# The last head group's values in two long bursts, on one core

## The chip, the cores and the metric

The kernel runs on one core of one Trainium2 chip. The metric is the time of one execution on the device, in microseconds (us). Three runs of the kernel before took 708.56 to 709.26 us, median 708.99.

## The reference

A sequence of 2048 rows of 512 numbers goes through two branches, which a gate mixes:

```
qkv = (x @ wqkv), 32 heads of 16
scores = q @ k.T / 4, kept where 0 <= query - key < 256
a = (softmax(scores) @ v) @ wo
b = (sigmoid(x @ w_gate) * (x @ w_up)) @ w_down        # 1376 hidden columns
g = sigmoid((x * gate_w).sum(-1))
out = g * a + (1 - g) * b
```

## The kernel before

**First phase.** The heads are taken in 8 groups of 4. The loop over `u` goes through 128 blocks of 128 rows (16 per group) and some more. At each `u`, four times (`hh`, one per head), TensorE multiplies a score tile with queries down the partitions (`s_part`), which VectorE scans for its row maxima, and nine blocks later (`LAG`) one with keys down the partitions (`st_part`), whose maxima are already in the operands, and which ScalarE turns into probabilities (`exps`). GpSimd masks the edges (`mask_p`). From `u` = 128 on there are no more score tiles to scan. Between them `turns` puts pieces of the gate, up and tail projections (`gu`, `tp`), pairs of half-array multiplications; the list `sizes` says how many pairs go into each gap. Where they end, VectorE transposes a tail result (`tail_post`) and the queue stores it.

**Values.** Groups 0 to 6 multiply probabilities with values in bursts, at every eighth `u` from 17 on (`pv_wide`): two steps of 512 queries, keys in halves of 64 so that half blocks outside the window are left out, into four PSUM banks (tags `pv`, `st`, `st`, `s`). Each step's two banks are then added: ScalarE copies one, VectorE adds the other. The last group (`u` from 121) is done otherwise: at `u` = 125, 129, 133 and 137 a visit (`pv_part`) multiplies one step with all 128 keys at once into the one bank `pv`, and ScalarE copies it (`o_take`). Its probabilities stand in `pbuf` alone, so that `pwide`, a part of the tile `V`, is free for loads of the second phase.

**PSUM.** The eight banks are shared by tag: `s` 2, `st` 2, `misc` 3, `pv` 1. A tile with a tag takes the bank that has been free longest.

**Second phase.** 44 steps (4 chunks of 512 rows, 11 of hidden columns): sigmoid on ScalarE, product on VectorE, a split in a high and a low part on both, 12 multiplications on TensorE. Step `n` reads what `h_load(n)` has brought to one of eight places of `V`; `H_LOAD` says at which `u` steps 0 to 6 are loaded, later ones seven steps ahead. `o_load` and `o_scale` bring the heads' outputs with the reciprocals of their sums (`rec_scratch`).

**Order.** TensorE, ScalarE, VectorE and the queue of transfers (SP) work in the order in which the code is written; the queue waits at a transfer until what it needs is done.

Of the kernel before, what the change touches and what calls it, by code (L numbers as in the profile page):

```python
# [43 lines left out]
NWIDE = NG - 1  # L44
# [3 lines left out]
GAPS = [3] * 12 + [2] * 3  # L48
# [11 lines left out]
SUMS = {129: 0, 131: 1, 134: 2}  # L60
# [5 lines left out]
H_LOAD = {126: (0,), 130: (1, 2), 134: (3, 4), 137: (5, 6)}  # L66
# [3 lines left out]
def gated_mix_kernel(  # L70
# [77 lines left out]
    with ExitStack() as actx:  # L148
# [225 lines left out]
        def s_part(u, hh):  # L374
            g, i = divmod(u, NB)
            s = g * NC + i // 4
            if i % 4 == 0 and hh == 0:
                mxs[s] = spool.tile([P, HG, 4], F32, tag="mx", name=f"mx{s}")
            k0 = max(0, i - 2)
            tag = "st" if u < LAG and hh >= 2 else "s"  # L380
            if PVLAG < u <= NB * NWIDE + LAG and (u - LAG) % WIDE == 0 and hh == 1:
# [46 lines left out]
        homes = (((0, 1), (9, 1), (3, 2), (4, 2)), ((0, 1), (3, 1), (9, 2), (10, 2)))  # L428

        def p_home(u):  # L430
            if u // NB >= NWIDE:
                s0, step = homes[u // 4 % 2][u % 4]
                return pbuf, 2 * s0, 2 * step
            w = u % WIDE
            if w < 5:
                return pbuf, 6 * w, 2
            return pwide, 24 if w == 5 else 12 * (u // WIDE % 2) + 6 * (w - 6), 2

        def p_blk(u, hh, a, n):
            buf, s0, step = p_home(u)  # L440
            if step == 2:
                return buf[:, s0 + 2 * a:s0 + 2 * (a + n), hh]
            pairs = buf.rearrange("p (s c) h t -> p s c h t", c=2)
            a = s0 // 2 + a * (step // 2)
            return pairs[:, a:a + (n - 1) * (step // 2) + 1:step // 2, :, hh]

        def p_run(u, hh, half, k, e):
            buf, s0, _ = p_home(u)
            return buf[HB * half:HB * half + HB, s0 + k:s0 + e, hh]

        def st_part(u, hh):
            g, j = divmod(u, NB)
            tag = "s" if u + LAG >= NU and hh >= 2 else "st"
            k8 = u % WIDE * HG + (hh ^ 1)
            if 2 <= u < NB * NWIDE and k8 % 3 == 1 and 4 <= k8 < WIDE * HG - 2:
                tag = "pv"
            pt = ps.tile([P, 3 * P], F32, tag=tag, name=f"st{u}_{hh}", bufs=1 if tag == "pv" else 2)
            lhsT = blk(g, j, hh, 1)
            last = min(NB, j + 3)
            for q, e in pieces(g, j, last):  # L460
# [5 lines left out]
            out = p_blk(u, hh, 0, n)  # L466
            seen = "p (k t) -> p k t" if len(out.shape) == 3 else "p (b k t) -> p b k t"
            exps.append(nc.scalar.activation(  # L468
                out, pt[:, 0:n * P].rearrange(seen, t=HB, **({} if len(out.shape) == 3 else {"k": 2})),
                AF.Exp, scale=SCALE,  # L470
            ))

        def mask_p(u):
            buf, s0, step = p_home(u)
# [4 lines left out]
            if u % NB + 2 < NB:  # L479
                old = buf[:, s0 + 2 * step:s0 + 2 * step + 2]  # L480
# [8 lines left out]

        def pv_part(s, bank):  # L490
            g, c = divmod(s, NC)
            q0 = 4 * c
            j0 = max(0, q0 - 2)
            for j in range(j0, q0 + 4):
                q, e = max(j, q0), min(j + 3, q0 + 4)
                for hh in range(HG):
                    v = (j * HG + hh) * VW
                    w = min(32, NB * HG * VW - v)
                    mm(
                        bank[32 * hh:32 * hh + w, (q - q0) * P:(e - q0) * P],  # L500
                        vt[:, v:v + w],
                        p_blk(g * NB + j, hh, q - j, e - q),
                        start=j == j0, stop=j == q0 + 3, skip_group_check=True,
                        tile_position=(0, 32 * hh),
                    )
# [30 lines left out]
        def o_take(s, bank):  # L536
            g, c = divmod(s, NC)
            ob = cpool.tile([P, CH], F32, tag="sp", name=f"ob{s}", bufs=5)
            nc.scalar.copy(ob, bank)
            for hh in range(HG):  # L540
                h = g * HG + hh
                later.append((oT_d[h * DH:(h + 1) * DH, c * CH:(c + 1) * CH], ob[32 * hh:32 * hh + DH]))
            later.append((sum_d[c, g * HG:(g + 1) * HG], ob.rearrange("(h r) f -> r h f", r=32)[DH]))

        def o_home(s):
            old = 12 * ((s // 2 + 1) % 2)
            return pwide[:, old:old + 4].rearrange("p c h t -> p (c h t)")

        def o_sum(s, n, banks):
            home = o_home(s)[:, n * CH:(n + 1) * CH]  # L550
# [4 lines left out]
        def o_store(s):  # L555
            g, c = divmod(s, NC)
            both = o_home(s)
# [222 lines left out]
        def turns():  # L780
# [3 lines left out]
            sizes = GAPS2 + GAPS2 * (NB * NWIDE // WIDE - 1) + GAPS2[:5] + GAPS[5:] + GAPS[0:12]  # L784
            sizes += [6] * 14
            for size in sizes:
                for _ in range(size):
# [4 lines left out]
                    for half, v in enumerate((t, t - SHIFT)):  # L792
                        if 0 <= v < n_rest * k3:
# [3 lines left out]
                            if k == 0 and n in ended and (size > 5 or len(exps) < ended[n] + 3):  # L797
                                after(ins, exps[ended[n]])
# [29 lines left out]

        def h_load(n):
            c, f = steps[n]  # L830
            if f < NFM:
                nc.sync.dma_start(hv[:, n % 8], gu_d[:, f, :, c * CH:(c + 1) * CH].rearrange("w p t -> p w t"))
# [26 lines left out]
        def h_src(n, w):  # L859
            c, f = steps[n]  # L860
            return (hv[:, n % 8, w] if f < NFM else tail_home(c, f, w))[0:FCH[f]]
# [32 lines left out]
        def sums_load(c):  # L894
            sm[c] = cpool.tile([P, D], F32, tag="draw", name=f"sm{c}", bufs=2)[:, 0:P]
            nc.sync.dma_start(sm[c], flat(sum_d, c))

        def sums_invert(c):
            t = sm.pop(c)
            nc.vector.reciprocal(t, t)  # L900
            return flat(rec_d, c), t
# [17 lines left out]

        U_WIDE = NB * NWIDE + LAG  # L920
# [7 lines left out]
        for u in range(N):  # L928
# [18 lines left out]
            def transfers():  # L947
                if mark and visits.get(u) != 2:
# [35 lines left out]
            for hh in range(HG):  # L984
                wide = visits.get(u) == 2
                if hh == 0 and u in visits:
                    s2 = (u - PVLAG) // 4 - wide
                    pv = ps.tile([P, CH], F32, tag="pv", name=f"pv{s2}", bufs=1)
                    if wide:
                        banks = [[pv], []]  # L990
                        for n, tag in ((0, "st"), (1, "st"), (1, "s")):
                            banks[n].append(ps.tile([P, CH], F32, tag=tag, name=f"pv{s2}_{tag}{n}", bufs=2))
                        pv_wide(s2, banks)
                    else:
                        pv_part(s2, pv)
# [10 lines left out]
                if hh == 0 and wide:  # L1006
# [4 lines left out]
                    max_load((u - 5) // 4)  # L1011
# [11 lines left out]
                elif hh == 0 and u in visits:  # L1023
                    evac.append(lambda s2=s2, pv=pv: o_take(s2, pv))
                if hh == 2 and mark:
                    transfers()
                long = LAG <= u < U_WIDE
# [11 lines left out]
                if hh == 0 and wide:  # L1039
# [43 lines left out]
            if u - 2 in SUMS:  # L1083
                behind.append(lambda c=SUMS[u - 2]: later.append(sums_invert(c)))
# [66 lines left out]
        for n, (c, f) in enumerate(steps):  # L1151
# [19 lines left out]
            if n == 3:  # L1171
                run_dmas(later)
                sums_load(NC - 1)
            if n == 6:
                last_sums = sums_invert(NC - 1)
            if n == 7:
                nc.sync.dma_start(*last_sums)
# [91 lines left out]
```

## Time and profile before

| | |
|---|---|
| median of 3 runs | 708.99 us |
| the profiled execution | 708.45 us, of it 706.5 us span |
| TensorE, VectorE, ScalarE busy | 99%, 71%, 62% |
| the last group's visits begin at | 491.86, 506.11, 518.98, 533.01 us |
| first multiplication of the second phase | 540.74 us |

Times in the trace are counted from the start of the span. A busy TensorE also holds the filling and emptying of its pipeline, so small stops are read from the starts of its instructions.

### The profile page before, as it was taken

Reading aid. Unit: us, or ns where it says so; the run is one execution under the profiler, and the core shown is the slowest. Engines: PE = TensorE matmul, PEld = TensorE weight load, DVE = VectorE, ACT = ScalarE, POOL = GpSimd, SP = SyncE. Lnnn points to the kernel's source line nnn. Section 1 sums busy time; section 2 is a strip of 40 time slices with the busy share of each in tenths; the row PEclk is TensorE's granted clock in tenths of the full one; section 3 lists DMA queues with packets and bytes.
Section 4 is the critical chain, followed back from the end, with each engine's and each line's share of the span. In section 5 each row is a group of like instructions: output and inputs, shape, how many; then the busy total and the mean of one; then the engine's idle time right before and its main releaser. Section 6 shows DMA issues by size and latency. Waiting matters only on the chain.

```text
span 706.5 us, 20062 instructions
## 1 busy us (share of the span) xinstructions
PE 702.5 (99%) x7545; PEld 608.8 (86%) x7545; DVE 498.6 (71%) x1486; ACT 435.3 (62%) x889; POOL 171.7 (24%) x254
## 2 busy tenths in 40 slices
PE   9999999999999999999999999999999999999998
PEld 7888889998899988889888988988888888888886
DVE  5368877777777776777777777786747768567481
ACT  6423777677677677767767767765676645435241
POOL 6200333233233233323323323332341000000000
PEclk9999999999999999999999999999999999999999
DMA  8466635646445365462655626664569969678531
GB/s 307 118 196 196 218 127 181 204 145 208 159 166 184 135 207 180 159 231 80 216 174 180 214 85 216 210 206 122 174 198 261 273 169 233 181 185 244 146 67 60
DMA packets 102832, 127.38 MB, mean 180 GB/s; under 512 B 45750, under 2 KB 62390, under 8 KB 102736
## 3 DMA queue, kind: packets, MB, share of 16 engines
q1 hardware_dynamic: 102592, 125.98, 58.3%
q8 instruction: 59, 0.97, 0.6%
q14 instruction: 37, 0.30, 0.1%
q10 hardware_dynamic: 144, 0.13, 0.1%
HBM read 71.80 MB, written 51.13 MB: 174 GB/s over the span
## 4 chain that ended last, share of the span: by engine, by line
PE 99%; DVE 0%; issue 0%
PE gu L296 29%; PE pj L296 12%; PE st L461 6%; PE s L386 6%; PE tp L687 6%; PE pd L99 5%; PE pd L98 5%; PE pd L100 5%; PE pv_st L516 4%; PE vh L724 4%; PE pv_s L516 3%; PE pa L98 2%; PE pa L100 2%; PE pa L99 2%; PE pv L516 2%; PE vps L586 2%
## 5 line engine op out<-in xcount | busy, mean ns | idle before, releaser
L392 DVE CUSTOM_DVE_ANT_0 junk<-s,mask 128x384 f32<-128x384 f32 (+2 forms) x512 | 271.8, 531 | 103.9 <-PE st L461 38.1
L296 PE MATMUL gu<-xh,w 64*128 64x512 f32 x1152 | 270.3, 391 | 0.0
L468 ACT ACTIVATE pbuf<-st 128x384 f32<-128x384 f32 (+2 forms) x344 | 165.5, 490 | 61.6 <-PE st L461 30.5
L296 PE MATMUL gu<-xl,w 64*128 64x512 f32 x576 | 182.4, 389 | 0.0
L461 PE MATMUL st<-ring 64*128 64x384 f32 (+2 forms) x536 | 164.7, 324 | 0.0
L386 PE MATMUL s<-ring 64*128 64x384 f32 (+2 forms) x536 | 162.9, 322 | 0.0
L296 PEld LDWEIGHTS gu<-xh,w 64*128 64x128 f32 x1152 | 151.2, 184 | 10.1
L475 POOL TENSOR_SCALAR_AFFINE_SELECT pbuf<-pbuf 128x512 f32<-128x512 f32 x86 | 58.1, 676 | 274.4 <-ACT pbuf L468 260.1
L386 PEld LDWEIGHTS s<-ring 64*128 64x128 f32 x536 | 94.8, 184 | 14.0 <-DVE mx L392 2.7
L461 PEld LDWEIGHTS st<-ring 64*128 64x128 f32 x536 | 95.8, 184 | 7.9 <-issue 1.2
L296 PEld LDWEIGHTS gu<-xl,w 64*128 64x128 f32 x576 | 88.6, 184 | 3.0
L468 ACT ACTIVATE V<-st 128x384 f32<-128x384 f32 (+2 forms) x168 | 72.2, 439 | 29.3 <-PE s L386 16.4
L296 PE MATMUL pj<-xl,wqh 64*128 64x512 f32 (+1 forms) x228 | 79.2, 389 | 0.0
L296 PE MATMUL pj<-xh,wqh 64*128 64x512 f32 (+1 forms) x228 | 79.2, 389 | 0.0
L296 PE MATMUL pj<-xh,wql 64*128 64x512 f32 (+1 forms) x228 | 69.6, 388 | 0.0
L99 PE MATMUL pd<-ring,hb 128*128 128x512 f32 x160 | 62.3, 389 | 0.0
L100 PE MATMUL pd<-ring,hb 128*128 128x512 f32 x160 | 62.3, 389 | 0.0
L98 PE MATMUL pd<-ring,hb 128*128 128x512 f32 x160 | 62.3, 389 | 0.0
L94 ACT CAST hb<-V 128x512 fp32r<-128x512 f32 x40 | 24.9, 622 | 58.3 <-DVE V L887 45.2
L481 POOL TENSOR_SCALAR_AFFINE_SELECT pbuf<-pbuf 128x512 f32<-128x512 f32 x84 | 56.0, 666 | 0.0
L647 ACT COPY sp<-gu 128x512 f32<-128x512 f32 x72 | 42.2, 586 | 9.6 <-PE gu L296 6.7
L475 POOL TENSOR_SCALAR_AFFINE_SELECT V<-V 128x512 f32<-128x512 f32 x42 | 27.8, 661 | 70.0 <-ACT V L468 49.2
(154 smaller groups left out, 1374.5 us busy)
## 6 DMA issues: line engine op xcount, KB each, us to landing
gu_scratch<-sp SPq DMA_DIRECT2D x72, 256.0 KB
V<-gu_scratch SPq DMA_DIRECT2D x36, 512.0 KB
ring<-stack_scratch SPq DMA_DIRECT2D x56, 256.0 KB
stack_scratch<-sh SPq DMA_DIRECT2D x14, 512.0 KB
stack_scratch<-sl SPq DMA_DIRECT2D x14, 512.0 KB
ring<-stack_scratch SPq DMA_DIRECT2D x14, 512.0 KB
guraw<-in_wgu_dram SPq DMA_DIRECT2D x18, 256.0 KB
v_scratch<-V SPq DMA_DIRECT2D x4, 1088.0 KB
```

The costliest lines, as they stand in the source:

```text
L98: mm(ps, lh, rh, start=first, stop=False)
L99: mm(ps, lh, rl, start=False, stop=False)
L100: mm(ps, ll, rh, start=False, stop=last)
L296: return mm(pt, (wl if w == 2 else wh)[r, d], (xl if w == 1 else xh)[r, d, c * CH:(c + 1) * CH], start=k == 0 and not second, stop=k == 3 ...
L386: mm(pt[:, (k - k0) * P:(e - k0) * P], lhsT, blk(g, k, hh, 1, e - k), start=k == k0, stop=e == i + 1, skip_group_check=True,)
L392: nc.vector.tensor_tensor_reduce(junk[:, 0:n], pt[:, 0:n], mask[:, 3 * P - n:], scale=1.0, scalar=NEG, op0=ALU.add, op1=ALU.max, accum_out ...
L461: mm(pt[:, (q - j) * P:(e - j) * P], lhsT, blk(g, q, hh, 0, e - q), start=q == j, stop=e == last, skip_group_check=True,)
L468: exps.append(nc.scalar.activation(out, pt[:, 0:n * P].rearrange(seen, t=HB, **({} if len(out.shape) == 3 else {"k": 2})), AF.Exp, scale=S ...
L475: nc.gpsimd.affine_select(buf[:, s0:s0 + 2], buf[:, s0:s0 + 2], pattern=[[HB, 2], [0, HG], [1, HB]], compare_op=ALU.is_ge, fill=0.0, base= ...
L481: nc.gpsimd.affine_select(old, old, pattern=[[-HB, 2], [0, HG], [-1, HB]], compare_op=ALU.is_gt, fill=0.0, base=0, channel_multiplier=1,)
L516: mm(bank[32 * hh:32 * hh + w, o + k * HB:o + e * HB], vt[HB * half:HB * half + HB, v:v + w], p_run(g * NB + j, hh, half, k, e), start=fir ...
L687: return mm(tp[b][:, 0:TW], (xl if w == 1 else xh)[r, d, b * P:(b + 1) * P], tw[d][int(w == 2)][r, 0:TW], start=k == 0 and not second, sto ...
```

## The change

The last group is treated as the others: a burst at `u` = 129 and one at `u` = 137 instead of four visits, its probabilities in `pbuf` and `pwide` as runs. The scores' banks follow the rule of the other groups up to `u` = 127, and the list of gaps runs on in the pattern of the other groups, then 9 gaps of 6 pairs and 6 of 5. The four steps of the maxima at `u` = 125 are spread over the gaps before it. The last burst's sums go to two tiles of their own. Since `pwide` is in use until the end, step 0 is loaded at `u` = 131, steps 1 and 2 at 134 and 135 into corners of the x tiles, steps 3 to 6 at 137 behind the burst; sums of steps 2 and 3 are inverted together in the second phase.

```diff
-NWIDE = NG - 1
-GAPS = [3] * 12 + [2] * 3
-SUMS = {129: 0, 131: 1, 134: 2}
+SUMS = {131: 0, 133: 1}
-H_LOAD = {126: (0,), 130: (1, 2), 134: (3, 4), 137: (5, 6)}
+H_LOAD = {131: (0,), 134: (1,), 135: (2,), 137: (3, 4, 5, 6)}
...
         def p_home(u):
-            if u // NB >= NWIDE:
-                s0, step = homes[u // 4 % 2][u % 4]
-                return pbuf, 2 * s0, 2 * step
...
         def st_part(u, hh):
-            tag = "s" if u + LAG >= NU and hh >= 2 else "st"
+            tag = "s" if u + LAG >= NU and hh % 2 else "st"
-            if 2 <= u < NB * NWIDE and k8 % 3 == 1 and 4 <= k8 < WIDE * HG - 2:
+            if 2 <= u < NU - LAG and k8 % 3 == 1 and 4 <= k8 < WIDE * HG - 2:
                 tag = "pv"
...
-            sizes = GAPS2 + GAPS2 * (NB * NWIDE // WIDE - 1) + GAPS2[:5] + GAPS[5:] + GAPS[0:12]
-            sizes += [6] * 14
+            sizes = GAPS2 * (NU // WIDE - 2) + GAPS2[:4 * (WIDE - 1)] + [6] * 9 + [5] * 6
...
+        def h_home(n, w):
+            if 0 < n < 3:
+                return slot(n - 1, w, 1).bitcast(F32)
+            return hv[:, n % 8, w]
...
-        visits = {u: 2 for u in range(PVLAG + 4, U_WIDE + 1, WIDE)}
-        visits.update({u: 1 for u in range(U_WIDE + 4, N, 4)})
+        visits = set(range(PVLAG + 4, N, WIDE))
...
             if n == 3:
                 run_dmas(later)
-                sums_load(NC - 1)
+                sums_load(NC - 2, 2)
```

On TensorE, at the border of `u` = 124 and 125, the kernel before has (s and st are the two kinds of score tiles, tp a tail projection, pv the visit):

```order
L386 MATMUL s_3_9176<-ring 128x384
L461 MATMUL st_2_9180<-ring 128x384
L499 MATMUL pv_9185<-pbuf,V 32x384 x8
L499 MATMUL pv_9185<-pbuf,V 32x256 x4
L499 MATMUL pv_9185<-pbuf,V 32x128 x4
L386 MATMUL s_0_9209<-ring 128x384
L461 MATMUL st_1_9213<-ring 128x384
```

and the change, at the same place of TensorE:

```order
L384 MATMUL s_3_9181<-ring 128x384
L446 MATMUL st_2_9185<-ring 128x384
L661 MATMUL tp_9061<-tail_hb_8620,xh 128x450
L661 MATMUL tp_9091<-tail_wqh_8168,xh 128x450
L661 MATMUL tp_9061<-tail_hb_8620,xl 128x450
L661 MATMUL tp_9091<-tail_wqh_8168,xl 128x450
L661 MATMUL tp_9061<-tail_hb_8620,xh 128x450
```

The visit between the scores is gone, and pairs of the tail projection follow at once.

TensorE's last visit (`u` = 137), between two tail groups, reads before:

```order
L499 MATMUL pv_9883<-pbuf,V 32x128 x4
L499 MATMUL pv_9883<-pbuf,V 32x256 x4
L499 MATMUL pv_9883<-pbuf,V 32x384 x8
L499 MATMUL pv_9883<-pbuf,V 32x256 x4
L499 MATMUL pv_9883<-pbuf,V 32x128 x3
L499 MATMUL pv_9883<-pbuf,V 17x128
```

and with the change it begins so (24 rows of four heads each in all):

```order
L482 MATMUL pv_9884<-V 32x192 x4
L482 MATMUL pv_st_9885<-V 32x256 x4
L482 MATMUL pv_9884<-V 32x64 x4
L482 MATMUL pv_9884<-pbuf,V 32x320 x4
L482 MATMUL pv_st_9885<-V 32x128 x4
L482 MATMUL pv_st_9885<-pbuf,V 32x320 x4
```

One step in one bank has become two steps, each in two banks for the two halves of the keys.

On the queue (SP), from the last loads of down weights on, before (wdraw is a down weight, xh and xl from tail_scratch are tail columns, V from gu_scratch is a step's load, here 5, 6 and 7):

```order
L132 DMA wdraw_9864<-in_wd_dram 96x512
L134 DMA wdraw_9864<-in_wd_dram 32x512
L358 DMA xl<-tail_scratch 32x16x32 x2
L832 DMA V<-gu_scratch 128x2x512 x3
L358 DMA xl<-tail_scratch 32x16x32 x2
L832 DMA V<-gu_scratch 128x2x512
L358 DMA xl<-tail_scratch 32x16x32 x2
```

and with the change, where the five loads are 3 to 7:

```order
L130 DMA wdraw_9865<-in_wd_dram 96x512
L132 DMA wdraw_9865<-in_wd_dram 32x512
L356 DMA tail_scratch<-tt_9881 128x448
L356 DMA xl<-tail_scratch 32x16x32 x2
L816 DMA V<-gu_scratch 128x2x512 x5
L356 DMA xl<-tail_scratch 32x16x32 x2
L816 DMA V<-gu_scratch 128x2x512
```

Two more loads of 512 KB, and a store of a tail result, stand ahead of what follows.

## Rows read from the trace of the kernel before

**Rows 1.** The page: busy time by engine; the chain that ended last, by engine.
```profile
PE 702.5 (99%) x7545; PEld 608.8 (86%) x7545; DVE 498.6 (71%) x1486; ACT 435.3 (62%) x889; POOL 171.7 (24%) x254
...
PE 99%; DVE 0%; issue 0%
```

**Rows 2.** Windows of two bursts and two visits: busy time, clock, DMA share, GB/s.
```profile
core 0: us, PE busy (x) PEld busy (x) DVE busy (x) ACT busy (x) POOL busy (x), PEclk, DMA share, GB/s
446.25:450.38 4.13, 4.13 (x162) 3.70 (x161) 3.55 (x9) 3.02 (x7) 1.72 (x2) 1.00 0.14 41
475.22:479.81 4.59, 4.59 (x195) 4.18 (x193) 2.11 (x8) 0.86 (x2) 0.66 (x1) 1.00 0.14 45
491.86:493.94 2.08, 2.08 (x35) 0.94 (x33) 2.01 (x9) 0.49 (x1) 1.27 (x2) 1.00 0.21 75
...
518.98:521.71 2.73, 2.73 (x51) 1.42 (x50) 1.23 (x4) 0.96 (x3) 1.32 (x2) 1.00 1.06 374
```

**Rows 3.** Timeline of PE around the third visit: start, duration, engine, line, instruction.
```profile
517.32 0.34 PE L461 MATMUL st<-ring 64*128 64x384 f32 x2
517.50 0.36 PE L687 MATMUL tp<-tail_wqh,xh 64*128 64x450 f32 x1
...
518.71 0.34 PE L461 MATMUL st<-ring 64*128 64x384 f32 x2
518.98 2.80 PE L499 MATMUL pv<-pbuf,V 128*32 128x128 f32 x48
...
521.99 0.36 PE L687 MATMUL tp<-tail_hb,xh 64*128 64x450 f32 x1
```

**Rows 4.** Timeline of DVE from the last burst to the third-last scan.
```profile
476.43 0.17 DVE L404 SCALAR_TENSOR_TENSOR nm<-mx,nm 128x16 fp32r<-128x16 f32 x1
...
488.71 0.56 DVE L392 CUSTOM_DVE_ANT_0 junk<-s,mask 128x384 f32<-128x384 f32 x1
...
489.42 0.56 DVE L392 CUSTOM_DVE_ANT_0 junk<-s,mask 128x384 f32<-128x384 f32 x1
...
490.16 0.56 DVE L392 CUSTOM_DVE_ANT_0 junk<-s,mask 128x384 f32<-128x384 f32 x1 [0.18 <-PE st L461]
...
493.35 0.50 DVE L404 SCALAR_TENSOR_TENSOR nm<-mx,nm 128x16 fp32r<-128x16 f32 x1
...
494.42 0.56 DVE L392 CUSTOM_DVE_ANT_0 junk<-s,mask 128x384 f32<-128x384 f32 x1 [0.32 <-PE st L461]
...
495.21 0.56 DVE L392 CUSTOM_DVE_ANT_0 junk<-s,mask 128x384 f32<-128x384 f32 x1 [0.22 <-PE s L386]
...
502.19 0.56 DVE L392 CUSTOM_DVE_ANT_0 junk<-s,mask 128x384 f32<-128x384 f32 x1
```

**Rows 5.** The last score on PE; waits from 480 to 506: total, times, longest.
```profile
503.27 0.34 PE L386 MATMUL s<-ring 64*128 64x384 f32 x1
...
PEld s L386 <- DVE mx L392: 0.7, 2, 0.3
```

**Rows 6.** Timeline of DVE: the two additions of the burst at 475.22.
```profile
478.49 0.69 DVE L553 TENSOR_TENSOR V<-pv_st,V 128x512 f32<-128x512 f32 x1 [1.64 <-ACT V L552]
...
480.81 0.69 DVE L553 TENSOR_TENSOR V<-pv_s,V 128x512 f32<-128x512 f32 x1
```

**Rows 7.** Timeline of the queue: start, time to issue.
```profile
527.57 0.34 SPq L896 DMA_DIRECT2D sm<-sum_scratch  x1
...
528.97 0.99 SPq L832 DMA_DIRECT2D V<-gu_scratch  x2
...
541.35 1.41 SPq L832 DMA_DIRECT2D V<-gu_scratch  x3
```

**Rows 8.** Timeline of DVE and of PE near the second phase's step 6.
```profile
553.35 0.01 DVE L1135 LOAD_MASK_SELECT spare<-xh  x1 [3.52 <-DMA xh<-rec_scratch]
...
554.72 0.68 DVE L95 TENSOR_TENSOR hb<-V,hb 128x512 fp32r<-128x512 f32 x1
...
557.07 0.39 PE L98 MATMUL pd<-ring,hb 128*128 128x512 f32 x1
```

**Rows 9.** Windows, columns as in rows 2: the first steps of the second phase.
```profile
541.00:560.00 19.00, 19.00 (x85) 15.74 (x84) 14.08 (x27) 11.57 (x22) 0.00 (x0) 1.00 0.92 240
```

More of the change, by code (lines that the diff above doesn't have):

```diff
@@ L426, in max_load @@
                 )
[L428 removed]
         def p_home(u):
[L431 to L433 removed]
             w = u % WIDE
             if w < 5:
[L436 to L445, printed above, removed]
+                return pbuf, 6 * w
+            return pwide, 24 if w == 5 else 12 * (u // WIDE % 2) + 6 * (w - 6)
         def p_run(u, hh, half, k, e):
[L448 removed]
+            buf, s0 = p_home(u)
             return buf[HB * half:HB * half + HB, s0 + k:s0 + e, hh]
@@ L465, in st_part @@
             n = last - j
-            out = p_blk(u, hh, 0, n)
-            seen = "p (k t) -> p k t" if len(out.shape) == 3 else "p (b k t) -> p b k t"
+            buf, s0 = p_home(u)
             exps.append(nc.scalar.activation(
-                out, pt[:, 0:n * P].rearrange(seen, t=HB, **({} if len(out.shape) == 3 else {"k": 2})),
-                AF.Exp, scale=SCALE,
+                buf[:, s0:s0 + 2 * n, hh], pt[:, 0:n * P].rearrange("p (k t) -> p k t", t=HB), AF.Exp, scale=SCALE,
             ))
         def mask_p(u):
-            buf, s0, step = p_home(u)
+            buf, s0 = p_home(u)
             nc.gpsimd.affine_select(
@@ L479, in mask_p @@
             if u % NB + 2 < NB:
-                old = buf[:, s0 + 2 * step:s0 + 2 * step + 2]
+                old = buf[:, s0 + 4:s0 + 6]
                 nc.gpsimd.affine_select(
@@ L534, in pv_wide, with o_home @@
                 sent[half] += pv_row(*rows[half].pop(0))
[L536 to L547, printed above, removed]
+        ohome = {}
+        def o_home(s, n):
+            if s < NSTEP - 2:
+                old = 12 * ((s // 2 + 1) % 2) + 2 * n
+                return pwide[:, old:old + 2].rearrange("p c h t -> p (c h t)")
+            if n not in ohome:
+                ohome[n] = cpool.tile([P, CH], F32, tag="sp", name=f"ob{n}", bufs=5)
+            return ohome[n]
         def o_sum(s, n, banks):
-            home = o_home(s)[:, n * CH:(n + 1) * CH]
+            home = o_home(s, n)
             some = slice(0 if (s + n) % NC else HB, CH)
@@ L556, in o_store @@
             g, c = divmod(s, NC)
-            both = o_home(s)
+            if s == NSTEP - 2:
+                for n in range(2):
+                    home = o_home(s, n)
+                    for hh in range(HG):
+                        h = g * HG + hh
+                        later.append((
+                            oT_d[h * DH:(h + 1) * DH, (c + n) * CH:(c + n + 1) * CH], home[32 * hh:32 * hh + DH]))
+                    later.append((
+                        sum_d[c + n, g * HG:(g + 1) * HG], home.rearrange("(h r) f -> r h f", r=32)[DH]))
+                return
+            old = 12 * ((s // 2 + 1) % 2)
+            both = pwide[:, old:old + 4].rearrange("p c h t -> p (c h t)")
             for hh in range(HG):
@@ L796, in turns @@
                             ins = groups[n][0](k, half, n in ended)
-                            if k == 0 and n in ended and (size > 5 or len(exps) < ended[n] + 3):
+                            if k == 0 and n in ended and (size > 4 or len(exps) < ended[n] + 3):
                                 after(ins, exps[ended[n]])
@@ L827, in gated_mix_kernel @@
         hv = Vf[:, 0:16 * CH].rearrange("p (n w t) -> p n w t", w=2, t=CH)
+        def h_home(n, w):
+            if 0 < n < 3:
+                return slot(n - 1, w, 1).bitcast(F32)
+            return hv[:, n % 8, w]
         def h_load(n):
             c, f = steps[n]
-            if f < NFM:
-                nc.sync.dma_start(hv[:, n % 8], gu_d[:, f, :, c * CH:(c + 1) * CH].rearrange("w p t -> p w t"))
+            if f >= NFM:
+                return
+            src = gu_d[:, f, :, c * CH:(c + 1) * CH]
+            if 0 < n < 3:
+                for w in range(2):
+                    nc.sync.dma_start(h_home(n, w), src[w])
+            else:
+                nc.sync.dma_start(hv[:, n % 8], src.rearrange("w p t -> p w t"))
         treads = {}
@@ L892, in flat, with sums_load, sums_invert @@
             return v[c].rearrange("h (q t) -> (h q) t", t=P)
[L894 to L898, printed above, removed]
+        def sums_load(c, n=1):
+            sm[c] = cpool.tile([P, D], F32, tag="draw", name=f"sm{c}", bufs=2)[:, 0:n * P]
+            for k in range(n):
+                nc.sync.dma_start(sm[c][:, k * P:(k + 1) * P], flat(sum_d, c + k))
+        def sums_invert(c, n=1):
             t = sm.pop(c)
             nc.vector.reciprocal(t, t)
-            return flat(rec_d, c), t
+            return [(flat(rec_d, c + k), t[:, k * P:(k + 1) * P]) for k in range(n)]
         def hold_group(step, _, post):
@@ L947, in transfers @@
             def transfers():
-                if mark and visits.get(u) != 2:
+                if mark and u not in visits:
                     run_dmas(later[:2])
@@ L984, in gated_mix_kernel @@
             for hh in range(HG):
-                wide = visits.get(u) == 2
                 if hh == 0 and u in visits:
-                    s2 = (u - PVLAG) // 4 - wide
+                    s2 = (u - PVLAG) // 4 - 1
                     pv = ps.tile([P, CH], F32, tag="pv", name=f"pv{s2}", bufs=1)
[L989 to L995, printed above, removed]
+                    banks = [[pv], []]
+                    for n, tag in ((0, "st"), (1, "st"), (1, "s")):
+                        banks[n].append(ps.tile([P, CH], F32, tag=tag, name=f"pv{s2}_{tag}{n}", bufs=2))
+                    pv_wide(s2, banks)
                 if hh and mid(u + 1):
@@ L1005, in gated_mix_kernel @@
                     max_store((u - 5) // 4)
-                if hh == 0 and wide:
+                if hh == 0 and u in visits:
                     flush(evac)
@@ L1022, in gated_mix_kernel @@
                     second_sum = o_sum(s2, 1, banks[1])
-                elif hh == 0 and u in visits:
-                    evac.append(lambda s2=s2, pv=pv: o_take(s2, pv))
                 if hh == 2 and mark:
                     transfers()
-                long = LAG <= u < U_WIDE
+                long = LAG <= u < NU
                 k8 = (u - LAG) % WIDE * HG + hh
@@ L1038, in gated_mix_kernel @@
                     part()
-                if hh == 0 and wide:
+                if hh == 0 and u in visits:
                     second_sum()
@@ L1083, in gated_mix_kernel @@
             if u - 2 in SUMS:
-                behind.append(lambda c=SUMS[u - 2]: later.append(sums_invert(c)))
+                behind.append(lambda c=SUMS[u - 2]: later.extend(sums_invert(c)))
             if u == TREAD:
```

28 lines of the change are left out of this document (6 added, 22 removed).

## The prediction, made before the change was run

> **What bounds the kernel now.** I read the page's busy shares and the chain that ended last first, then the trace in stretches. TensorE is busy 99% of the span and the chain runs through it for 99% [rows 1]. Such a busy figure hides small stops, so the question for each stretch is which engine sets TensorE's pace. The change touches the stretch from 479.8 us (the end of the last two-step burst of the old kind) to 557 us, where the second phase has begun. The values of the last group are multiplied there in four visits, which begin at 491.86, 506.11, 518.98 and 533.01. Rows 2 time the first and the third, and two bursts of the kind that replaces them: one visit is 2.08 long, and 2.73 stands for three that are alike. The clock is granted in full in all of them (1.00).
>
> **The multiplication itself.** Four visits cost 2.08 + 3 x 2.73 = 10.27 us. A burst over the first two steps of a head took 4.13 and one over the last two 4.59 [rows 2], 8.72 together, because half blocks skip what the window masks: 1.55 less. Entering and leaving a visit costs more: a pair of score multiplications is followed by the next instruction after 0.18 us (517.32 to 517.50) where nothing switches, after 0.27 where a visit begins (518.71 to 518.98), and the second instruction behind one stands 0.28 after the first (521.71, the visit's end in rows 2, to 521.99) [rows 3]. That is 0.19 per visit, and two visits fewer save 0.38. TensorE's own account is thus 1.93 us. The group's other multiplications are the same in number: the table of turns moves them between the gaps and adds none.
>
> **Who uses the time of the first visit.** The visit at 491.86 is also a pause for VectorE, which must scan each score tile for its maximum before TensorE can write that bank again. Its rows show it [rows 4]. Scans that follow without a wait stand 0.71 us apart (488.71 to 489.42), and the one at 490.16 had to wait a little (idle 0.18), so there VectorE was level with TensorE. From then on it has no idle time until 494.42 (0.32) and 495.21 (0.22): both just behind the visit, in which it was busy 2.01 of 2.08 us [rows 2]. Afterwards it shows no idle time over its usual 0.15 between scans up to the third-last scan, at 502.19. TensorE has two score banks there, so its last score (503.27) cannot come before the third-last scan has ended, and it already stood twice behind a scan for 0.7 us in all [rows 5].
>
> With the visit gone, the same sequence has to be done by VectorE: from 490.16 to the end of the third-last scan, 502.19 + 0.56 = 502.75, are 12.59 us. Of these I take away the two idle times over the usual gap, 0.54 - 2 x 0.15 = 0.24, and 0.33 by which one small step on the maxima took longer during the visit (0.50) than elsewhere (0.17) [rows 4], since the change spreads these steps over three slots. The order of VectorE's instructions up to that scan is otherwise the same in number and kind: three tail transposes, one down-weight split. That leaves 12.02 us, so the third-last scan ends near 502.18, and the last score can move from 503.27 only to 502.18. **The first visit's 2.27 us (2.08 + 0.19) give back 1.09.** If VectorE were no bound, the gain here would be those 2.27, and at most 0.7 more, the wait there now; if the steps on the maxima save nothing, it is 0.76, and the floor is 0.
>
> **The sum**, place by place, as the gain at the end of each:
> - the visit at 491.86 goes: +1.09 (0 to 2.97)
> - the visit at 506.11 becomes a burst: 2.73 - 4.13 = -1.40
> - the visit at 518.98 goes: 2.73 + 0.19 = +2.92; VectorE is free there, and nothing waits for it
> - the last one becomes a burst: 2.73 - 4.59 = -1.86
>
> Together +0.75 us (-0.34 to 2.63). The profiled execution took 708.45 us with a span of 706.5, 0.54 under the median of the runs shown, which is 708.99; the same difference from that gives **708.2 us**.
>
> **What else is added.** A burst leaves four banks to empty where a visit leaves one: one copy on ScalarE and one addition on VectorE more per two steps. At the burst of 475.22 the additions ran at 478.49, inside the burst, and at 480.81, when the next scores were already being multiplied, from the burst's end at 479.81 [rows 2, 6]; I cost them at nothing because the burst and the two untouched buffers of scores cover them. Uncovered, the later one would cost its 0.69 at each of two bursts. The Trainium skill, in TensorEngine Tiling (Array Packing), section PSUM Bottleneck, says that packing the array speeds up TensorE but not the emptying of PSUM; by it two uncovered additions would turn the sum into a loss of 0.63 us. The row at 480.81 does not bear that out for the additions. The strided homes of the probabilities become plain runs of the buffer, with the same element counts per exponential; nothing is gained or lost by that in the sum.
>
> **The loads.** Step 0 is loaded later, steps 1 and 2 go to two free corners of the x buffers, and the loads of steps 3 to 6, two of which were issued at 528.97, now stand behind the last burst, together with those of 5 and 6, in front of step 7's. They cannot run before the burst has read the probabilities under them. In the kernel before, the queue issued loads 5, 6 and 7 at 541.35 [rows 7], 5.6 us after the last visit's end, since transfers filled it. What is late next is not a load but what is queued behind: the row of reciprocals for the first output block. VectorE waited 3.52 us for it, until 553.35, and did step 6's low half only at 554.72 to 555.40; TensorE began step 6 at 557.07 [rows 8], so there is 1.67 us to spare, 0.92 after a gain of 0.75. Two loads of 512 KB at 240 GB/s [rows 9] are 4.4 us. I cost this at nothing for a reason in the queue: the stores of the visit at 518.98 and the sums that wait for them, which held the queue up to 527.57, are gone from that place, loads 1 and 2 take the transfers' time of the old loads 3 and 4, and the queue should reach the last burst's end (near 535.0) some 5 us earlier than 541.35. Without that, 4.4 - 0.92 = 3.5 us are lost.
>
> **The rivals.**
> - *VectorE is no bound.* The first visit gives back all of its 2.27: 1.93 us in all, 707.1, and down to 706.4 if the wait of 0.7 goes too. For it: VectorE's busy share is 71% over the span [rows 1], and its scans may be fed more evenly. Against it: 12 us without idle time in rows 4.
> - *The row of reciprocals comes late* (slower). The queue is as late as before, 541.35, and TensorE waits 3.5 us at step 6: 711.7. It decides when the queue reaches load 3 later than some 538 us. For it: transfers were the limit there (0.92 of 16 engines busy [rows 9]). Against it: the list that must go out before is no longer, and starts sooner.
> - *ScalarE binds the end of the first phase.* The last six gaps have 5 turns instead of 6, beside two exponentials and a split each; some tenths each, at most 1 us: about 709.2, no change.
>
> **How the numbers follow.** What a measurement of this kernel can tell from no change is about 0.2%, 1.4 us. VectorE binds, as summed: 0.48. No bound: 0.32, nearly all of it over 1.4 us of gain. Late row: 0.14, slower. ScalarE: 0.06. So faster 0.33, same 0.53, slower 0.14. The likeliest case is 708.2, between 707.5 (the wait of 0.7 gone as well) and 709.3 (the first visit gives nothing back); the range takes in the first rival to its end, 706.4, and most of the way to the second, 710.6.
>
> **What would show it.** Right: behind the burst at 479.8 VectorE's scans follow at 0.71 without idle time from about 490 to 503, TensorE's weight loads for scores wait for VectorE there more often than the 0.7 us of now, and the burst that takes the second visit's place begins near 505; the two new bursts last 4.1 and 4.6 us; no sigmoid and no multiplication of the second phase waits for a load. Wrong: that burst begins before 504 (no bound), steps 3 to 7 show gaps on TensorE (loads or the row late), or the new bursts stand on masks of GpSimd, which the sum takes as in time.

## The result and the profile after

The change makes the kernel slower: 711.83 us (median of nine, 710.41 to 714.25) against 709.26 (nine, 708.35 to 709.90) for the kernel before; the ratio is 1.0045, with a 95% interval of 1.003 to 1.006. I had forecast 708.2 against 708.99, a gain of 0.75; it is a loss of 2.57. The profiled execution took 712.36 us, with a span of 710.6.

The page after, in the lines that answer to [rows 1]:

```profile
PE 703.0 (99%) x7721; PEld 607.3 (85%) x7721; DVE 500.9 (70%) x1489; ACT 435.6 (61%) x889; POOL 171.3 (24%) x254
...
PE 97%; DMA 1%; issue 1%; DVE 0%; ACT 0%; DVEq 0%
```

TensorE's busy time has hardly moved, but its part of the chain fell from 99% to 97%: it now stops. Where, the windows of the three bursts tell (the second and third are the new ones; columns as in [rows 2]):

```profile
core 0: us, PE busy (x) PEld busy (x) DVE busy (x) ACT busy (x) POOL busy (x), PEclk, DMA share, GB/s
475.80:480.29 4.49, 4.49 (x194) 4.15 (x192) 2.11 (x8) 0.86 (x2) 0.66 (x1) 1.00 0.14 46
505.49:509.52 4.03, 4.03 (x162) 3.64 (x160) 2.81 (x7) 1.47 (x4) 1.72 (x2) 1.00 0.44 136
532.19:536.32 4.13, 4.13 (x164) 3.49 (x164) 2.00 (x5) 1.27 (x3) 0.00 (x0) 1.00 0.99 256
536.32:538.57 2.25, 0.16 (x4) 0.00 (x0) 0.00 (x0) 0.00 (x0) 0.00 (x0) 1.00 1.00 307
538.57:539.25 0.68, 0.68 (x29) 0.52 (x28) 0.00 (x0) 0.00 (x0) 0.00 (x0) 1.00 0.78 223
```

The last burst is torn: after 164 multiplications TensorE stands for 2.25 us and then does the last 29. No other engine works in that time, only the DMA engines (share 1.00). The timeline of PE at that place:

```profile
536.11 0.38 PE L482 MATMUL pv_st<-V 64*32 64x256 f32 x1
538.57 0.41 PE L482 MATMUL pv_st<-V 64*32 64x256 f32 x3 [2.09 <-issue]
```

The releaser is "issue": the engine waited for nothing that the profile shows. The DMA view from 536.1 to 537.1 shows what else went on:

```profile
q1 hardware_dynamic: 302, 0.36, 100.1%
q8 instruction: 1, 0.02, 5.5%
```

One packet of TensorE's instruction queue moves there (16 KB, from 536.15 to 537.03), among 302 packets of data.

The waits of TensorE's weight loads after, from 480.3 to 505.5 (the first line) and from 509.52 to 532.19 (the others; total, times, longest):

```profile
PEld s L384 <- DVE mx L390: 2.7, 9, 0.9
...
PEld tp L661 <- ACT V L452: 0.7, 2, 0.5
...
PEld st L446 <- ACT V L452: 0.3, 1, 0.3
```

In the first stretch VectorE is waited for nine times, where it was two [rows 5]; in the second ScalarE's exponentials are late, and the kernel before shows no such wait in this stretch (508.74 to 533.01). One reason, in this profile, is a cast that waits for a down weight:

```profile
528.06 0.62 ACT L138 CAST ring<-wdraw 128x512 fp32r<-128x512 f32 x1 [0.70 <-DMA wdraw<-in_wd_dram]
```

**The account, place by place**, from the starts and ends of TensorE's multiplications (shifted windows aside, the same places as in my sum). Burst to burst or visit: 26.40 before, 25.20 after, so +1.20. The second visit, 2.63, became a burst of 4.03: -1.40. The stretch to the last visit: 24.27 before (with the third visit in it), 22.67 after: +1.60. The last visit, 2.63, became 7.06, with the stop in it: -4.43. The stop is all that is new in it: the last multiplication ahead of the stop starts 3.92 after the burst's first, and the same one of the burst at 475.80 does so too. In all the last burst takes 7.06 - 4.49 = 2.57 longer than that one; the window above counts 2.25 of them as the stop. Together the places give -3.03. The profile after was already 0.58 later at 475.80, where the code had not changed; with that it is 3.61, and step 0 of the second phase begins at 544.34 instead of 540.74, 3.60 later. From there to the last multiplication nothing more is lost or won (706.64 against 703.04).

### The profile page after: what moved, and what is told of

Its sections match the earlier page's. It is cut to its first block, busy times and chain, and to the rows that moved or that the text cites. A ratio compares the mean times of both kernels' runs of the same rounds, so it can differ in the third digit from the quotient of the medians.

```text
span 710.6 us, 20438 instructions
## 1 busy us (share of the span) xinstructions
PE 703.0 (99%) x7721; PEld 607.3 (85%) x7721; DVE 500.9 (70%) x1489; ACT 435.6 (61%) x889; POOL 171.3 (24%) x254
## 4 chain that ended last, share of the span: by engine, by line
PE 97%; DMA 1%; issue 1%; DVE 0%; ACT 0%; DVEq 0%
PE gu L294 28%; PE pj L294 12%; PE s L384 6%; PE st L446 6%; PE pd L97 5%; PE pd L98 5%; PE pd L96 5%; PE pv_st L482 5%; PE tp L661 4%; PE vh L698 4%; PE pv_s L482 3%; PE pv L482 2%; PE pa L96 2%; PE pa L98 2%; PE pa L97 2%; PE vps L560 2%
## 5 line engine op out<-in xcount | busy, mean ns | idle before, releaser
L452 ACT ACTIVATE pbuf<-st 128x384 f32<-128x384 f32 x320 | 155.4, 494 | 53.7 <-PE st L446 25.9
L446 PE MATMUL st<-ring 64*128 64x384 f32 (+2 forms) x536 | 166.4, 325 | 0.1
L458 POOL TENSOR_SCALAR_AFFINE_SELECT pbuf<-pbuf 128x512 f32<-128x512 f32 x80 | 53.3, 666 | 263.9 <-ACT pbuf L452 248.4
L452 ACT ACTIVATE V<-st 128x384 f32<-128x384 f32 (+2 forms) x192 | 81.9, 439 | 32.4 <-PE s L384 16.3
L464 POOL TENSOR_SCALAR_AFFINE_SELECT pbuf<-pbuf 128x512 f32<-128x512 f32 x80 | 52.9, 661 | 0.0
L458 POOL TENSOR_SCALAR_AFFINE_SELECT V<-V 128x512 f32<-128x512 f32 x48 | 31.8, 662 | 79.4 <-ACT V L452 54.6
```

The costliest lines, as they stand in the source:

```text
L446: mm(pt[:, (q - j) * P:(e - j) * P], lhsT, blk(g, q, hh, 0, e - q), start=q == j, stop=e == last, skip_group_check=True,)
L452: exps.append(nc.scalar.activation(buf[:, s0:s0 + 2 * n, hh], pt[:, 0:n * P].rearrange("p (k t) -> p k t", t=HB), AF.Exp, scale=SCALE,))
L458: nc.gpsimd.affine_select(buf[:, s0:s0 + 2], buf[:, s0:s0 + 2], pattern=[[HB, 2], [0, HG], [1, HB]], compare_op=ALU.is_ge, fill=0.0, base= ...
L464: nc.gpsimd.affine_select(old, old, pattern=[[-HB, 2], [0, HG], [-1, HB]], compare_op=ALU.is_gt, fill=0.0, base=0, channel_multiplier=1,)
```

## The experiments

**The change once more, unchanged.**

> The changed kernel again, unchanged. Theory A (the stop of 2.25 us inside the last burst is TensorE waiting for its own instructions, which are fetched late because transfers fill the DMA engines): the stop comes again at about the same place of the last burst, 1 to 3 us long, since the transfers beside it are the same; ratio to the kernel before 1.003 to 1.006. Theory B (the stop was an accident of one profiled execution and the loss lies elsewhere, in the gaps with five turns and behind the burst): no stop in the last burst, and the ratio is still 1.003 to 1.006.

711.69 us against 709.49, ratio 1.0039 (1.0027 to 1.0052). Its profile, in windows of the last burst:

```profile
530.98:535.11 4.13, 4.13 (x164) 3.49 (x164) 1.99 (x4) 1.16 (x2) 0.00 (x0) 1.00 1.00 246
535.11:536.50 1.39, 0.16 (x5) 0.00 (x0) 0.00 (x0) 0.00 (x0) 0.00 (x0) 1.00 0.91 301
536.50:537.18 0.68, 0.68 (x29) 0.53 (x28) 0.00 (x0) 0.00 (x0) 0.00 (x0) 1.00 0.95 256
```

The stop is there again, behind the same 164 multiplications, but 1.39 long (this profile is of the fastest of the six executions, 710.29). Theory A stands, B falls.

**A burst that never stopped, under extra transfers** (the kernel before, with this ahead of its burst at 475 us):

```diff
+            if u == 120:
+                for k in range(6):
+                    nc.sync.dma_start(extra_d[k], wgu[k])
```

> The kernel before with six transfers of 512 KB more (weights copied to a scratch in DRAM that nothing reads), issued behind u = 120, ahead of the burst that begins near 475 us and that never stopped. Theory A: that burst now stops inside, between two of its multiplications, for 0.5 to 3 us, with no releaser shown, and a 16 KB packet of TensorE's instruction queue starts late in it. If a stop needs something of the last burst itself (its rows, masks, banks), this burst stays at 4.5 us without a stop, and only TensorE's waits for transferred rows grow behind it.

It stops, for 3.87 us:

```profile
479.92 0.29 PE L517 MATMUL pv_s<-V 64*32 64x64 f32 x3
483.92 0.42 PE L517 MATMUL pv_s<-V 64*32 64x64 f32 x5 [3.71 <-issue]
```

The instruction packet began at 481.55, after TensorE had stopped. This burst works on other rows and stopped at another place (five multiplications before its end), so the stop belongs to the transfers, not to the last burst. This is one execution, and the only one of this kernel. The windows around it show a second price:

```profile
475.30:480.05 4.75, 4.75 (x192) 4.37 (x191) 2.39 (x8) 0.92 (x3) 0.66 (x1) 1.00 1.00 340
480.05:483.92 3.87, 0.16 (x14) 0.06 (x1) 0.00 (x0) 0.59 (x1) 0.00 (x0) 0.83 1.06 404
483.92:486.00 2.08, 2.08 (x14) 1.91 (x15) 0.90 (x3) 0.49 (x1) 0.00 (x0) 0.50 0.42 132
486.00:489.00 3.00, 3.00 (x19) 2.72 (x18) 1.40 (x5) 1.05 (x3) 0.00 (x0) 0.50 0.08 18
```

The granted clock falls within the idle time (0.83 on the mean) and is 0.50 (1.2 GHz) until 489. The one time is 715.5 us.

**Fewer transfers beside the burst.** First only the small reads are moved behind it:

```diff
-            if u >= TREAD:
-                tail_read(0, 2)
...
-                tail_read(c, 2)
+                tail_read(c, 2 if c else 4)
```

> The ten reads of tail columns (pieces of 128 bytes) that ran beside the last gaps and the last burst are issued behind the burst, four per step. Theory A: fewer transfers between 524 and 541 us, so TensorE's instructions come in time; the stop shrinks from 2.25 us to under 0.7, and the ratio falls from 1.0045 to 1.001 to 1.003. Theory C (the burst waits for something that its rows read, masks or exponentials, or is slow in itself): the stop stays at 2 us or more and the ratio at 1.0045. If the reads are now late for step 9, sigmoids there wait for them and the ratio rises instead.

The stop shrank to 0.49, as theory A had it, but the time rose: 715.01 against 709.49, ratio 1.0084 (1.0071 to 1.0097). The loss came back in the second phase, where the moved reads delay the row of reciprocals (VectorE waited 4.0 us for it) and with it a low half for TensorE (1.4 us at 567). Then the reads are left out, with two loads:

```diff
-H_LOAD = {131: (0,), 134: (1,), 135: (2,), 137: (3, 4, 5, 6)}
+H_LOAD = {131: (0,), 137: (3, 4, 5, 6)}
...
-            if u >= TREAD:
-                tail_read(0, 2)
...
-            if f < 4:
+            if f < 4 and c:
```

> The change without loads 1 and 2 and without the fourteen reads of tail columns of the first output block (steps 1, 2, 9 and 10 then use what lies there, so part of the computation is left out). Theory A: no stop over 0.3 us in the last burst and no wait over 0.5 us in the second phase; 0.5 us above the kernel before, ratio 1.0005 (0.999 to 1.002). Rival D: stop and ratio as in the change, 1.004.

710.03 us, ratio 1.0015 (1.0006 to 1.0024), ten times between 709.61 and 711.01. The stop is 0.31 and no load is late. Rival D falls: by the medians two thirds of the loss hang on these transfers, through the stop and the late loads together; this run does not part the two.

**Loads earlier, by two tables.**

```diff
-H_LOAD = {131: (0,), 134: (1,), 135: (2,), 137: (3, 4, 5, 6)}
+H_LOAD = {130: (0,), 131: (1, 2), 137: (3, 4, 5, 6)}
```

> The change with loads 0, 1 and 2 issued 4 to 10 us earlier (behind u = 130 and 131, not 131, 134 and 135), to the same places; DMA stands idle at 514 to 517 us. Theory A (late instructions; the transfers beside the last burst cause it, and what remains comes out as late loads): 1 MB leaves the stretch 526 to 537, the stop in the last burst falls under 0.7 us, loads 3 to 7 are issued near 537 instead of 540 to 541, and no step of the second phase waits over 0.5 us. By the places (1.20 and 1.60 given back, 1.40 and 1.86 spent) the time is 0.5 us above the kernel before: ratio 1.0005, at most 1.002. Rival D (the loads have nothing to do with it, the burst stops by itself): stop 1.4 to 2.3 us as in the two profiles of the change, ratio 1.004.

712.3 us, ratio 1.0044 (1.0027 to 1.006). The stop in the profile is 0.45, but the loads now stand in front of a down weight: ScalarE's cast waited 1.5 us for it, and a weight load of TensorE 1.14 us for the exponential behind that, until 531.16. The stop is short, but this is the slowest of the six executions (714.22). My 1.0005 was wrong; the transfers only changed places. The next version sent loads 3 and 4 ahead as well, to a third corner:

```diff
+H_LOAD = {130: (0,), 131: (1, 2), 135: (3, 4), 137: (5, 6)}
...
+            if 3 <= n < 5:
+                return slot(0, 2 * (n - 3) + w, 2).bitcast(F32)
```

> As the run with three loads earlier, and loads 3 and 4 go into the corner of the x buffers that the tail multiplications leave at u = 135, before the last burst, so that only 5 and 6 stand behind it. Theory A: the second phase has still more room, but 1 MB comes back beside the last burst; the stop is between none and 2.2 us, no step of the second phase waits, ratio 1.000 to 1.003. Rival D: 1.004.

714.08 us, ratio 1.0065 (1.0043 to 1.0087), worse than expected, with the cast's wait (1.6 us) and a stop of 2.78.

**Corners swapped**, so that the loads and reads can run where the DMA engines had little to do (a share of 0.24 from 514 to 517 in the change), and nothing is left out:

```diff
-TREAD = 133
+TREAD = 128
-H_LOAD = {131: (0,), 134: (1,), 135: (2,), 137: (3, 4, 5, 6)}
+H_LOAD = {127: (1,), 128: (2,), 130: (0,), 137: (3, 4, 5, 6)}
...
-        wo_h = [slot(0, d, 0) for d in range(ND)]
+        wo_h = [slot(0, d, 1) for d in range(ND)]
...
-                return slot(n - 1, w, 1).bitcast(F32)
+                return slot(n - 1, w, 0).bitcast(F32)
```

> The change with two corners of the x buffers swapped: loads 1 and 2 and the reads of tail columns go where the first four tail multiplications end (u = 125), the output weights where the next four end (u = 131). So the loads are issued behind u = 127 and 128, the fourteen reads from u = 128 on, load 0 behind u = 130; nothing is left out. Theory A: TensorE's instructions come in time, stop in the last burst under 0.5 us, loads 3 to 7 issued right behind the burst, no wait over 0.5 us in the second phase; ratio as in the run with less read, 1.0015 (1.000 to 1.0025). If it stays at 1.004, the transfers are not what costs the change its time.

The profile is as expected (stop 0.53, no wait in the second phase), the times are not: 712.6 us, ratio 1.0047 (1.0034 to 1.006), from 711.48 for the profiled execution up to 713.7. One profile does not speak for executions whose stop may be longer.

**One group of slow instructions inside the burst:**

```diff
+            half_way = sum(map(len, rows)) // 2
             while rows[0] or rows[1]:
+                if s == NSTEP - 2 and sum(map(len, rows)) == half_way:
+                    hold_group(*rest.pop(0))
```

> The change with one of the two held groups of twelve tail multiplications moved from behind the last burst into its middle; the transfers stay. The group takes about 2.4 us with 24 instructions, where the burst takes 4.1 us with 384 or fewer, so TensorE uses its instructions more slowly. Theory A: the stop is gone or under 0.7 us, ratio 1.001 to 1.003. A rival by which TensorE stops at a fixed place of the burst whatever comes before it: the stop stays 2 us long at the same multiplication, ratio 1.0045.

No stop in the profile, though the DMA share was 1.13 in both halves, and yet 712.27 us, ratio 1.0038 (1.0025 to 1.0052). That profile shows small waits for late halves at 568 (0.41 and 0.59). So either remedy alone leaves the median where it was.

**The halves of the change.** The last burst cut into two visits:

```diff
-        visits = set(range(PVLAG + 4, N, WIDE))
+        visits = {u: 2 for u in range(PVLAG + 4, N - 8, WIDE)}
+        visits.update({N - 5: 1, N - 1: 1})
```

> Half of the change: the burst at 505 us stays, the last burst is cut into two visits of one step each (at u = 133 and 137), the gaps have six turns again; the loads stay as in the change. By the terms of my sum (2.92 given back at the third visit, 1.86 lost at the last burst) this must be 1.06 us slower than the whole change: 712.9, ratio 1.006. By what the two traces showed (1.60 given back, 4.43 lost) it is 2.8 us faster: 709.0, ratio 1.0005. No stop inside a visit.

714.62 us, ratio 1.0076 (1.0061 to 1.0092): neither number. There is no stop in a visit, but now the second rival of my prediction strikes: the five loads still stand behind the last visit, and go out at 544.19, where the change had 541.44. The profile is of the slowest of the six executions (717.51). In the queue, VectorE and TensorE:

```profile
544.19 2.49 SPq L843 DMA_DIRECT2D V<-gu_scratch  x5
...
560.09 0.01 DVE L1148 LOAD_MASK_SELECT spare<-xh  x1 [3.36 <-DMA xh<-rec_scratch]
...
562.19 0.50 PE L98 MATMUL pd<-ring,hb 128*128 128x512 f32 x1 [2.22 <-DVE hb L93]
```

The row of reciprocals comes at 560.09, and step 6 waits 2.22 us. The clock follows again, at 0.62 on the mean behind the wait:

```profile
562.19:566.65 4.46, 4.46 (x12) 3.53 (x13) 4.25 (x8) 3.96 (x7) 0.00 (x0) 0.62 0.86 253
```

So this run doesn't tell the halves apart. A cleaner one: the first burst alone in the kernel before, with as many loads ahead of the last visit as there, and with the change's rules for the scores' banks and the gaps up to it (some lines left out).

```diff
-            if u // NB >= NWIDE:
+            if u >= NU - WIDE:
...
+        visits = {u: 2 for u in range(PVLAG + 4, N - 8, WIDE)}
+        visits.update({N - 5: 1, N - 1: 1})
...
-H_LOAD = {126: (0,), 130: (1, 2), 134: (3, 4), 137: (5, 6)}
+H_LOAD = {129: (0,), 130: (3, 4), 134: (1, 2), 137: (5, 6)}
```

> The first half of the change alone: the visits at 491.86 and 506.11 become one burst, the last two visits stay, with their rows' homes as in the kernel before, and with as many loads ahead of the last visit as there (0, 3 and 4 before 1 and 2). By the two traces this gives back 1.20 and costs 1.40: 0.2 us slower, ratio 1.0003 (0.999 to 1.0015). If the first half already carries the loss, the ratio is 1.003 or more.

710.0 us, ratio 1.0011 (1.0002 to 1.002): by the medians the first half carries a quarter of the loss, and the rest comes with the second.

**Who holds the gaps.** VectorE's low halves left out in the first stretch:

```diff
-        behind.append(low) if late else low()
+        (f > 3) and (behind.append(low) if late else low())
```

> The change without the low halves of the first four splits of the down weights (VectorE subtractions near 487 to 503 us, left out of the computation). If VectorE sets the pace between the bursts at 476 and 505 us, as the prediction says, that stretch shrinks from 25.20 us by 0.7 or more (at most by the 2.7 that TensorE lost in it), and the weight loads for scores wait less for VectorE than the 2.7 us they did. If TensorE or ScalarE sets it, it stays within 0.2 of 25.20.

The stretch fell from 25.20 to 24.60, and the waits for scans from 2.7 to 2.1 us. It is VectorE, though four subtractions of 0.69 bought only 0.60, a little less than I asked for. (Its one execution took 712.09 us; the last burst stopped for 2.78.) The last gaps the other way round:

```diff
-[6] * 9 + [5] * 6
+[5] * 6 + [6] * 9
```

> The change with the six gaps of five turns put first and the nine of six turns last, so that the gaps in which ScalarE was late (from 523 us) are longer. If ScalarE's lateness there is what kept the third visit's 2.92 us from coming back in full, the stretch from the burst at 505 us to the last burst loses less idle time than the 1.6 to 2.1 us of the change's profiles, by 0.5 to 1.0 us, and the ratio falls from 1.004 to about 1.003. If it is not, the stretch stays at 22.1 to 22.7 us. The stop in the last burst stays (1.4 to 2.8 us), since the transfers beside it stay.

711.5 us, ratio 1.0033 (1.002 to 1.0045). The stretch took 21.91, where the repeat of the change had 22.13 and its first profile 22.67, so 0.22 to 0.76 less where I asked for 0.5 to 1.0; the weight loads' waits for exponentials fell from 1.0 to 0.2, and the stop stayed (1.92). With corners swapped too:

> Both of it: corners swapped, and the gaps of six turns last. If the two causes are apart from each other, the gains add: ratio 0.999 to 1.0015.

711.61 us, ratio 1.0035 (1.0019 to 1.0051), from 708.89 to 714.32. The gains did not add: in its profile the stop is 0.64, but the stretch took 22.90, with ScalarE's casts waiting 1.6 us for down weights, so the moved transfers may cost there what the gaps gave.

**Three remedies at once, and the floor.** Corners swapped, sixes last, and the group inside:

> Corners swapped, gaps of six turns last, and one held group inside the last burst. Theory A: no stop over 0.3 us in the last burst in any execution, so the spread narrows and the ratio is 1.000 to 1.002. If the loss lies in the schedule of the gaps and bursts and not in late instructions, the ratio stays at 1.0035.

709.85 us, ratio 1.0011 (1.0002 to 1.002), eleven times between 709.27 and 710.96. Its windows of the last burst, with the group between the halves:

```profile
532.56:534.89 2.33, 2.33 (x97) 1.96 (x96) 1.29 (x3) 0.67 (x2) 0.00 (x0) 1.00 1.03 334
534.89:537.63 2.74, 2.74 (x21) 2.19 (x13) 0.00 (x0) 0.59 (x1) 0.00 (x0) 1.00 0.72 236
537.63:540.12 2.49, 2.49 (x97) 1.80 (x96) 1.29 (x3) 0.00 (x0) 0.00 (x0) 1.00 0.30 106
```

No idle time, and the spread is gone. (Corners and group without the new order of the gaps were not run.) And without the transfers:

> As the run with less read (loads 1, 2 and fourteen reads left out of the computation), with the gaps of six turns last. If ScalarE's lateness in the short last gaps is the rest of the loss (0.6 us in the repeat's profile), the ratio falls from 1.0015 to 1.0005 to 1.001; if not, it stays at 1.0015.

709.61 us, ratio 1.0004 (0.9995 to 1.0013): with these loads and reads left out and the gaps in the better order the change costs nothing that can be measured, and still gains nothing. TensorE still pauses for some 0.3 us behind the same 164 multiplications. The step from 1.0015 is 0.8 us, about what ScalarE's lateness was worth; the two intervals overlap.

The packets of TensorE's instruction queue beside the stops, out of each trace (us):

```
run                       packet             resumes  end to resume  stop
change, first profile     536.15 to 537.03   538.57   1.54           2.25
e0_repeat                 533.43 to 535.30   536.50   1.20           1.39
e1_reads_behind           534.32 to 535.27   536.61   1.34           0.49
e4_three_earlier          537.43 to 539.02   540.47   1.45           0.45
e5_five_earlier           537.74 to 538.72   540.01   1.29           2.78
e7_fewer_splits           536.00 to 536.96   538.23   1.27           2.78
e8_sixes_last             534.90 to 535.86   537.19   1.33           1.92
e9_corners_swapped        535.22 to 536.17   537.64   1.47           0.53
e10_swapped_sixes_last    535.21 to 536.27   537.64   1.37           0.64
e6_less_read              533.86 to 534.92   536.38   1.46           0.31
e11_extra_transfers       481.55 to 482.51   483.92   1.41           3.87
```

TensorE goes on 1.20 to 1.54 us after its packet's end, whatever the stop's length, in all eleven. That ties the two together. Nor are the packets slow: they take 0.88 to 1.86 us, and 0.88 to 1.54 at the other places between 440 and 575 us in the profiles of the change and of the kernel before. In the long stops they begin late. Why one begins late beside a full load of transfers, no row shows.

## Why the prediction was wrong

**The step that failed** is "the last one becomes a burst: 2.73 - 4.59 = -1.86". It cost 4.43 in the profile and 3.57 in the repeat (6.20 - 2.63). I took a burst's length from two bursts with a DMA share of 0.14 [rows 2] and set it beside a share of 0.99. Up to the stop the burst ran as I had it, so what the step lacked is the stop alone: 2.57 and 1.71. A burst works through TensorE's instructions fast, 386 multiplications and weight loads in 4.49 us where the 22.67 us before the last one have 397, and the packets that bring them are moved by the same DMA engines; none of my rivals had this. Shown: extra transfers cause the stop in another burst, and the stop's end follows the packet.

**"The visit at 518.98 goes: +2.92; VectorE is free there, and nothing waits for it"** was mis-sized: it gave 1.60, in the repeat 2.14. VectorE was free, but ScalarE's exponentials came late once the pause was gone: TensorE's weight loads waited 1.0 us for them, in the repeat 0.7; the kernel before shows no such wait. It is my third rival, costed at 1 us at most; it came with the stop, not instead of it. Sixes last gave part back; what holds the rest (21.91 against 24.27 - 2.92 = 21.35) stays open.

**The first visit** was right, 1.20 for 1.09: scans at 0.71 without idle time, TensorE at their pace. Two of them after the change:

```profile
500.43 0.56 DVE L390 CUSTOM_DVE_ANT_0 junk<-s,mask 128x384 f32<-128x384 f32 x1
...
501.14 0.56 DVE L390 CUSTOM_DVE_ANT_0 junk<-s,mask 128x384 f32<-128x384 f32 x1
```

So was the second, -1.40, as forecast. The additions were covered: behind the last burst the second one runs at 540.11, and TensorE shows no wait there.

**The loads** I costed at nothing for a wrong reason. The queue reached load 3 at 541.44, not near 536; for 1.2 us of that it held a down weight until load 2, which I had sent ahead, was there:

```profile
541.44 2.70 SPq L816 DMA_DIRECT2D V<-gu_scratch  x5
...
556.96 0.01 DVE L1113 LOAD_MASK_SELECT spare<-xh  x1 [2.83 <-DMA xh<-rec_scratch]
```

The row came at 556.96, 3.61 later than before [rows 8]; 1.67 were to spare, and TensorE did not wait because it was itself 3.60 late. The second rival's 711.7 lies close to the result by luck: its wait at step 6 is not in the profile. That a late row does cost time when no stop comes first, the cut burst shows (2.22 us, with loads later still); the small waits of the group inside (0.41 and 0.59) fit it. This may be why either remedy alone helped so little. In both, executions up to 713.7 remain, which were not profiled; the two slowest have a mean granted clock of 0.998 with the corners swapped and 0.999 with the group inside, and which of the two losses they had stays open.

Open is also why the first burst alone costs 0.8 us where the change's places say 0.2 (the interval holds 0.2 at its edge). No version here beats the kernel before.

## What to carry to other kernels

Take a burst's length from a place with the same DMA share, and ask how fast it uses up instructions: many short multiplications in a stretch where transfers fill the DMA engines can stop TensorE with no releaser shown. When a pause goes, look at every engine that caught up in it, not only the one that binds elsewhere. And where one delay hides another, removing one shows nothing; remove both before you judge.

## What the runs showed that I had not expected

TensorE's instruction queue moved 61 packets of 16 KB in the change's profile, for 7,721 multiplications and as many weight loads: some 253 instructions each (it is by this count that I take the queue q8 for TensorE's). The Trainium skill, in Runtime: NRT & Kernel Launch (Instruction fetch mechanics), says that instructions come in such blocks over a DMA queue of their own, and that the cost of a block's border is mostly hidden. The trace agrees with the block's size; the second part did not hold in the last burst beside a DMA share of 0.85 to 1.01, where it cost 0.45 to 2.78 us, nor under the extra transfers (3.87). The share alone does not set the length: the stop of 2.78 came at 0.85 and at 1.01, the one of 0.53 at 0.97.

After a stop of 3.87 us and a wait of 2.39 (the cut burst's step 6) the granted clock fell to 0.50 (1.2 GHz), in the first until 489; after the change's 2.25 and 1.39 us it stayed at 1.00. The length alone does not decide it: of two stops of 2.78 at the same place of the last burst, the clock fell after one (five loads earlier: 0.65 from 541 to 545 us) and stayed at 1.00 after the other (fewer splits). This bears on the spread: of the change's nine executions the three slowest (713.86 to 714.25) have a mean granted clock of 0.998, the other six (up to 712.36) 0.999 or 1.000, so the slowest lost clock as well. That a longer stop was the cause there is likely, but not shown, since they were not profiled.
